# A remade order for the opening list of a fused attention and feed-forward kernel on one Trainium2 core

## The chip, the cores and the metric

The kernel runs on one core of one Trainium2 chip. The metric is the device time of one execution in microseconds (us); lower is better. The engines are TensorE (PE, with its weight loads as PEld), VectorE (DVE), ScalarE (ACT), GpSimd (POOL) and the sync engine (SP), which here only issues transfers (DMA). Each engine works through its own instructions in order.

## The reference

The kernel computes attention within chunks of 64 tokens, and on its result a feed-forward layer with a leaky rectifier:

```python
scores = scale * np.matmul(q_c, k_c.transpose(0, 1, 2, 4, 3))   # chunks of 64 x 64, scale = 1/8
scores = scores - np.max(scores, axis=-1, keepdims=True)
attn = np.exp(scores)
attn = attn / (np.sum(attn, axis=-1, keepdims=True) + 1e-09)
out = np.matmul(attn, v_c)                                      # 8 x 8 heads x 576 x 64
x = out.transpose(0, 2, 1, 3).reshape(4608, 512)
h = x @ w_in                                                    # 512 x 2048
g = np.maximum(h, 0.0) + alpha * np.minimum(h, 0.0)
y = g @ w_out                                                   # 2048 x 512
```

All inputs are float32. The weights w_in and w_out reach the chip as 64-bit floating point numbers, split in the kernel into 32-bit parts.

## The kernel before, in words

The 4608 tokens are cut into 36 sub-blocks of 128 tokens (two chunks, eight heads), and four sub-blocks form a block of 512 tokens. Every operand of a large product is kept as two parts, a high one rounded to TensorE's fp32r form and a low one, the rest; a product is then high by high, high by low and low by high. The first three blocks go through the feed-forward layer directly, the other six in pairs by a scheme with seven products instead of eight on quarters of the matrices (lines 588 to 871), for which combinations of the weights are made and stored on the way.

The change is in the opening of the kernel. There the attention of the first eight sub-blocks (0 to 3 form block 0, 4 to 7 block 1), the conversion of the first nine of sixteen slices of both weights, and the first feed-forward steps of blocks 0 and 1 are issued in an order that is written out by hand: the string `START` (line 28), whose tokens the function `start` (line 879) turns into instructions one after the other. Within `tc.manual_schedule` (line 930) each engine keeps exactly the order of the tokens that belong to it. After the list a scheduler orders the instructions; the TensorE order is fixed again from step 20 on (line 957).

A token is a letter or two and a number. For sub-block s:

- `q`, `k`, `v`: a load (line 544, 552). Two sub-blocks at a time from s = 2 on. q0 and q1 are issued by ScalarE, the others by SP. The room for q and k of 4 and 5 is that of 0 and 1, so that this load waits for S0 and S1.
- `S`: scores, 16 small fp32 products into PSUM (line 256). `m`: their maxima on VectorE (line 298). Then, in the usual way, `z` scales the maxima (a small VectorE operation, line 309), `e` is 16 instructions on ScalarE, eight exponentials with the maximum as bias and eight reads of the accumulated sum (line 313), and `a` adds 1e-9 to the sums on GpSimd. For a sub-block in `SUBTRACTED`, `z` subtracts the maxima from the scores on VectorE (line 302), `e` is one exponential over the whole sub-block (line 304), and `a` is a sum on VectorE and the addition (line 307, 317). `r` is the reciprocal, `n` the multiplication with it (line 321, 323).
- `T`: four transposes on TensorE (line 344), `p`: the copy out of PSUM on ScalarE (line 356). `V`: the product with v, 16 small products (line 360); `x`: the high part of x, a copy on ScalarE (line 373); `l`: its low part, a subtraction on VectorE (line 375).
- `W`: that many products of zeros (128x128) on TensorE (line 895); nothing reads them.

For a weight slice f, `wi` or `wo` with the number alone is the load of 512 KB (line 178, SP). The following letters are the steps of its conversion (`piece`, line 180): `b` the magnitude (ScalarE, for `wi0` VectorE), `k`, `h`, `u`, `v` four integer steps on VectorE, `i` the high part (ScalarE, for `wi0` VectorE), `j` the low part (VectorE). `HALVES` names the scratch tile of each slice.

For block b and slice f, `h` is the first layer's 12 products of 128x512 (line 416), `R` a Relu on ScalarE, `G` the rectify on VectorE, `gh` the high part on ScalarE, `gl` the low part on VectorE, and `o` the second layer's 12 products (line 450). So h00 is block 0, slice 0, and o16 block 1, slice 6. `K` copies one of block 0's four partial results out and stores it (line 467). The first block's first turn takes three slices, the second's nine (`TURNS`, line 91): h18, h03 and so on follow after the list.

`BANKS` says which PSUM banks S, T and V of a sub-block use: before, one of three pairs of banks (ps_a, ps_oa, ps_ob); T uses the first bank of a pair.

Of the kernel before, what the change touches and what calls it, by code (L numbers as in the profile page):

```python
# [19 lines left out]
def bits(pattern):  # L20
# [5 lines left out]


START = """
W8 q0 k0 k1 q1 q2 S0 W1 k2 m0 S1 W5 wi1 z0 m1 e0 wi0 z1 a0 e1 r0 S2 k4 n0 S3 m2 q4 wi1b z2 T0 W6 m3
e2 a1 z3 wi1k v0 wi0b r1 wi1h n1 wi2 p0 wi0k T1 a2 e3 wi0h r2 S4 W3 v2 wi0u n2 m4 q6 p1 V0 a3 z4  # L30
wi0v e4 T2 W4 k6 r3 wi0i wi1u wi0j wo4 wi1v x0 V1 n3 p2 wo0 l0 x1 V2 wi2b a4 l1 T3 x2 wo1 wi2k S5 p3
l2 wi1i V3 m5 v6 S6 r4 x3 z5 n4 e5 wi4 l3 h00 m6 v4 wi2h z6 wi1j e6 wi2u S7 wi3 a5 wi2v h01 m7 wo2
r5 R00 z7 n5 wo0b G00 wi5 wi2i T5 e7 wo0k wi2j h02 wi7 a6 wo0h r6 wo0u wo5 n6 p5 wo0v gh00 T6 wo1b
a7 T4 wo3 gl00 wo0i V5 r7 wo1k p6 wo0j x5 V6 n7 p4 l5 x6 T7 wo1h V4 l6 p7 wo1u x4 o00 R01 wo1v wo2b
G01 wo1i l4 gh01 wo1j R02 V7 gl01 o01 x7 wo2k G02 wi4b wi3b wo2h wo2u gh02 l7 h10 wo2v gl02 wo2i
wi3k wo2j wi4k wo4b o02 wi3h wi4h R10 wo4k wi4u K0 wi3u K1 G10 h11 wi4v gh10 wi3v wi4i gl10 K2 wi3i
wo4h wi4j K3 o10 wo4u wo5b wi3j R11 wo4v wi5b G11 wo4i wo6 h12 wo5k gh11 wo4j wi6 gl11 wo3b wo5h
wo3k wo5u wo8 o11 R12 wo3h wo5v wi8 G12 wo5i wo3u gh12 wo7 h13 wo5j gl12 wi7b wo3v wi5k wo3i wi7k
wi5h o12 R13 wo3j wi5u G13 wi5v gh13 h14 wi7h wi5i gl13 wi6b wi5j wi6k wi7u wi6h o13 R14 wi7v G14
wi7i wi6u gh14 wo6b wi6v h15 gl14 wi6i wo6k wi6j wi7j wo7b wo6h o14 wo7k R15 wo6u G15 wo6v gh15 wo7h  # L40
wi8b gl15 h16 wo6i wo7u wo7v wo6j wo7i wi8k o15 wo7j R16 wo8b G16 wi8h gh16 wi8u gl16 h17 wi8v wo8k
wi8i wi8j wo8h o16 R17 G17 wo8u gh17 wo8v gl17 wo8i wo8j
"""
# [12 lines left out]
LISTED = 18

# [2 lines left out]
def tile_local_attention_prelu_ffn(  # L60
# [63 lines left out]
    def place(name, shape, dtype):  # L124
        return sides[name[:2]][0].tile(shape, dtype, name=name)
# [15 lines left out]
    FREE = 12  # L141
    RAWS = 6
# [89 lines left out]
    def attn_load(s, parts="qkv"):  # L232
# [61 lines left out]
    def early_softmax(s, sc3):  # L294
# [412 lines left out]
    banks = ["ps_h", "ps_h", "ps_o0", "ps_o1", "ps_o2", "ps_o3"]  # L707
# [171 lines left out]
    def start(token):  # L879

        name, at = re.fullmatch(r"([a-zA-Z]+)(\d+)([a-z]?)", token).group(1, 2)
        s = int(at)
        if name in ("wi", "wo"):
            if token[-1].isdigit():
                fetch(name, s)
            elif token[-1] == "b":
                running[name, s] = piece(name, s, f"{name}{s}" in ALONE)
                next(running[name, s])
            else:
                next(running[name, s])  # L890
        elif name in ("q", "k"):
            first(("q", "k").index(name), s, 1 if s < 2 else 2, nc.scalar if token in ("q0", "q1") else nc.sync)
        elif name == "v":
            first_v(s)
        elif name == "W":
            hps = ps_h.tile([P, TB], F32, name="ps_h")
            for _ in range(s):
                nc.tensor.matmul(hps[:, :P], lhsT=plain, rhs=plain, start=True, stop=True)  # L898
        elif name == "S":
            running["softmax", s] = early_softmax(s, early_scores(s))  # L900
        elif name in ("m", "z", "c", "e", "a", "r", "n"):
            next(running["softmax", s])
        elif name == "T":
            running["transpose", s] = early_transpose(s)
            next(running["transpose", s])
        elif name == "p":
            next(running["transpose", s])
        elif name == "V":
            running["values", s] = early_values(s)
            next(running["values", s])  # L910
        elif name in ("x", "l"):
            next(running["values", s])
        elif name == "K":
            store(accs[0], 0, True, (s,))
        else:
            b, f = int(at[0]), int(at[1:])
            if name == "h":
                running["ffn", b, f] = first_layer(x[b], f)
                next(running["ffn", b, f])
            elif name in ("R", "G", "gh"):  # L920
                next(running["ffn", b, f])
            elif name == "gl":
                scored[b, f] = next(running["ffn", b, f])
            elif name == "o":
                if f == 0:
                    accs[b] = results()
                ffn_out(accs[b], scored.pop((b, f)), f, 0, (n0, n1)[b] - 1)
# [153 lines left out]
```

## Time and profile before

| | us |
|---|---|
| median of three runs | 770.79 |
| lowest and highest run | 770.68, 771.45 |
| span of the profiled execution | 770.2 |
| TensorE busy in it | 760.4 (99%) |
| VectorE busy | 646.7 (84%) |
| ScalarE busy | 447.3 (58%) |
| GpSimd busy | 184.8 (24%) |

The span goes from the first to the last instruction; of the profiled execution no other time is given than this span, which lies 0.6 us under the median of the runs. A busy share is an average over the whole span. Matmuls overlap, so that a row's duration (0.38 us for a 128x512 product) is longer than the distance from one to the next.

### The profile page before, as it was taken

The numbers are of one execution on the slowest core, as the hardware profiler recorded it, in microseconds if no ns is written. First come the engines' busy times: TensorE is split into PE (matmuls) and PEld (weight loads), VectorE is DVE, ScalarE is ACT, GpSimd is POOL, SyncE is SP. The second block draws the span as 40 slices with busy tenths as digits, with TensorE's granted clock in tenths as the row PEclk, the third lists the DMA queues.
The fourth block names the chain that finished last, engine by engine and source line by source line (L and its number), as shares of the span: only waits on it lengthen the run. The fifth ranks groups of instructions, "written<-read, shape, count | busy, mean of one in ns | idle before, by whom it ended". The sixth has DMA issues, their size and how long they took to land.

```text
span 770.2 us, 15415 instructions
## 1 busy us (share of the span) xinstructions
PE 760.4 (99%) x5558; PEld 639.8 (83%) x5558; DVE 646.7 (84%) x1140; ACT 447.3 (58%) x1221; POOL 184.8 (24%) x304
## 2 busy tenths in 40 slices
PE   7999999999999999999999999999999999999998
PEld 7788887888888888888888888888888888888886
DVE  6999988989899886877899898777898977679784
ACT  6975555576666665666657456664574544354643
POOL 1153322343254331111121121111221121122110
PEclk9999999999999999999999999999999999999999
DMA  9859496468798775878765678875656765555573
GB/s 349 337 196 386 176 324 216 163 229 226 234 238 274 240 258 200 304 275 277 263 234 197 233 250 288 269 239 206 207 193 223 260 228 193 204 205 192 198 258 144
DMA packets 69322, 184.52 MB, mean 240 GB/s; under 512 B 10992, under 2 KB 18176, under 8 KB 69120
## 3 DMA queue, kind: packets, MB, share of 16 engines
q0 software_dynamic: 34336, 119.56, 45.9%
q1 hardware_dynamic: 34480, 63.20, 24.2%
q8 instruction: 44, 0.72, 0.4%
q10 hardware_dynamic: 432, 0.79, 0.3%
q14 instruction: 30, 0.25, 0.1%
HBM read 135.27 MB, written 42.99 MB: 231 GB/s over the span
## 4 chain that ended last, share of the span: by engine, by line
PE 92%; ACT 4%; DVE 2%; DMA 2%; issue 0%; ACTq 0%; SPq 0%
PE ps_o L722 20%; PE ps_o L850 19%; PE ps_h L422 14%; PE ps_h L722 10%; PE ps_h L850 10%; PE ps_oa L458 8%; PE ps_ob L458 7%; PE ps_a L388 2%; PE ps_a L272 2%; ACT wi L313 1%; ACT wo L313 1%; DMA raw<-w_in 1%; DMA raw<-w_out 1%; PE ps_h L898 1%; ACT wi L207 0%
## 5 line engine op out<-in xcount | busy, mean ns | idle before, releaser
L422 PE MATMUL ps_h<-xh,wi 128*128 128x512 f32 x384 | 101.7, 385 | 0.7 <-DVE g L410 0.5
L422 PEld LDWEIGHTS ps_h<-xh,wi 128*128 128x128 f32 x384 | 70.7, 187 | 13.8 <-DVE g L410 0.9
L722 PE MATMUL ps_o<-wi,raw 128*128 128x512 f32 x336 | 79.1, 382 | 0.0
L722 PEld LDWEIGHTS ps_o<-wi,raw 128*128 128x128 f32 x336 | 62.5, 187 | 11.2
L678 ACT CAST gh<-wo 128x512 fp32r<-128x512 f32 x66 | 41.0, 620 | 47.4 <-PE ps_o L850 31.8
L287 ACT ACTIVATE pr<-ps_a,mx 128x64 f32<-128x64 f32 x224 | 67.2, 325 | 0.8
L458 PE MATMUL ps_oa<-wo,gh 128*128 128x512 f32 x192 | 58.5, 385 | 0.1
L458 PE MATMUL ps_ob<-wo,gh 128*128 128x512 f32 x192 | 57.7, 380 | 0.0
L422 PE MATMUL ps_h<-xl,wi 128*128 128x512 f32 x192 | 50.6, 381 | 0.0
L679 DVE TENSOR_TENSOR gl<-wo,gh 128x512 fp32r<-128x512 f32 x63 | 43.2, 686 | 7.5 <-ACT gh L678 7.1
L287 ACT ACTIVATION_READ_ACCUMULATOR pr<-ps_a,mx 128x1 f32 x224 | 48.6, 217 | 0.0
L659 POOL DMA_DIRECT2D raw<-wi_a x42 | 22.3, 531 | 102.1 <-PE ps_o L722 54.5
L659 POOL DMA_DIRECT2D raw<-wo_a x42 | 22.2, 529 | 90.8 <-PE ps_o L850 51.2
L407 ACT ACTIVATE wo<-gh 128x512 f32<-128x512 f32 x24 | 15.2, 632 | 48.5 <-DVE gh L752 48.5
L678 ACT CAST ta<-wo 128x512 fp32r<-128x512 f32 x42 | 26.1, 621 | 26.4 <-PE ps_o L850 15.2
L422 PEld LDWEIGHTS ps_h<-xl,wi 128*128 128x128 f32 x192 | 35.8, 187 | 6.7 <-DVE xl L375 0.2
L458 PEld LDWEIGHTS ps_ob<-wo,gh 128*128 128x128 f32 x192 | 35.9, 187 | 6.4
L458 PEld LDWEIGHTS ps_oa<-wo,gh 128*128 128x128 f32 x192 | 35.3, 187 | 7.0 <-ACT gh L436 0.5
L722 PE MATMUL ps_o<-wi,wo 128*128 128x512 f32 x168 | 40.4, 383 | 0.0
L722 PE MATMUL ps_o<-wi,wi 128*128 128x512 f32 x168 | 40.4, 383 | 0.0
L722 PE MATMUL ps_h<-wi,raw 128*128 128x512 f32 x168 | 40.4, 382 | 0.0
L407 ACT ACTIVATE g<-ps_h 128x512 f32<-128x512 f32 x48 | 29.5, 614 | 17.5 <-PE ps_h L422 17.5
(296 smaller groups left out, 2036.2 us busy)
## 6 DMA issues: line engine op xcount, KB each, us to landing
raw<-wi_a POOLq DMA_DIRECT2D x42, 512.0 KB, 4.4
raw<-wo_a POOLq DMA_DIRECT2D x42, 512.0 KB, 3.5
wi<-wi_a POOLq DMA_DIRECT2D x21, 512.0 KB, 3.7
wo<-wi_a POOLq DMA_DIRECT2D x21, 512.0 KB, 4.3
wi<-wo_a POOLq DMA_DIRECT2D x21, 512.0 KB, 3.5
wo<-wo_a POOLq DMA_DIRECT2D x21, 512.0 KB, 3.6
k_sb<-kT SPq DMA_DIRECT2D x28, 256.0 KB, 4.7
q_sb<-qT SPq DMA_DIRECT2D x28, 256.0 KB, 4.1
```

The source lines that it names most:

```text
L272: pe(nc.tensor.matmul(att[0][c * C:(c + 1) * C, par, (NP + hp) * C:(NP + hp + 1) * C], lhsT=q_sb[rows, 2 * hp + c], rhs=kb[rows, 2 * hp + ...
L287: last = nc.scalar.activation(pr[:, g], sc3[:, g // NP, g % NP], AF.Exp, bias=mx[:, g], scale=SCALE, accum_out=sm[:, g])
L313: last = nc.scalar.activation(pr[:, g], sc3[:, g % 2, g // 2], AF.Exp, bias=mx[:, g], scale=SCALE, accum_out=sm[:, g])
L388: pe(nc.tensor.matmul(att[0][par * C:(par + 1) * C, c, hp * C:(hp + 1) * C], lhsT=v_sb[rows, h * C:(h + 1) * C], rhs=p[rows, :, par * NP + ...
L407: nc.scalar.activation(g, h, AF.Relu, scale=-1.0)
L422: pe(nc.tensor.matmul(woven(hps), lhsT=wi[f][:, l, k * P:(k + 1) * P], rhs=woven(xx[:, k]), start=(i == 0 and k == 0), stop=(i == 2 and k ...
L458: pe(nc.tensor.matmul(woven(o), lhsT=a[:, ts], rhs=woven(wo[f][:, l]), start=(f == first and i == 0), stop=(f == last and i == 2),))
L659: streamed[0] = nc.gpsimd.dma_start(out=f32(t), in_=units[side][n])
L678: hi = nc.scalar.copy(t_hi, t)
L679: return hi, nc.vector.tensor_tensor(t_lo, t, f32(t_hi), op=ALU.subtract)
L722: pe(nc.tensor.matmul(woven(ps), lhsT=w[:, l, k * P:(k + 1) * P], rhs=woven(xx[:, xl]), start=first and at == 0, stop=at == n - 1, skip_gr ...
L850: pe(nc.tensor.matmul(woven(ps[m]), lhsT=w[:, l, m * P:(m + 1) * P], rhs=woven(xx), start=i in (1, 5, 2) and j == 0 and n == 0, stop=j == ...
```

## The change

The list gets another order. Eight products of zeros (W8) stand in front as before, but of the later ones 7 are left of 19. `SUBTRACTED` now holds sub-blocks 0, 2, 5 and 6 instead of 0 alone. For the sub-blocks in the new `REMAINDERS` (0 to 4), the low part of x is formed in PSUM: the high part, once copied out, is multiplied by a negated identity on TensorE and added to the bank (a new token `X`, two products of 128x256), and `l` is then a copy on ScalarE. The identity is negated once, on ScalarE. `BANKS` now counts single banks (a pair is two numbers), T may use either bank of a pair or a bank of ps_h (6 and 7), and one tile per pair serves all tokens. `HALVES` is remade with the order. The lists are cut here to the front, and the new one to the front, the middle that bears on block 1, and the end.

```diff
 START = """
-W8 q0 k0 k1 q1 q2 S0 W1 k2 m0 S1 W5 wi1 z0 m1 e0 wi0 z1 a0 e1 r0 S2 k4 n0 S3 m2 q4 wi1b z2 T0 W6 m3
-e2 a1 z3 wi1k v0 wi0b r1 wi1h n1 wi2 p0 wi0k T1 a2 e3 wi0h r2 S4 W3 v2 wi0u n2 m4 q6 p1 V0 a3 z4
-wi0v e4 T2 W4 k6 r3 wi0i wi1u wi0j wo4 wi1v x0 V1 n3 p2 wo0 l0 x1 V2 wi2b a4 l1 T3 x2 wo1 wi2k S5 p3
-l2 wi1i V3 m5 v6 S6 r4 x3 z5 n4 e5 wi4 l3 h00 m6 v4 wi2h z6 wi1j e6 wi2u S7 wi3 a5 wi2v h01 m7 wo2
...
-wi8b gl15 h16 wo6i wo7u wo7v wo6j wo7i wi8k o15 wo7j R16 wo8b G16 wi8h gh16 wi8u gl16 h17 wi8v wo8k
-wi8i wi8j wo8h o16 R17 G17 wo8u gh17 wo8v gl17 wo8i wo8j
+k0 q0 W8 S0 m0 k1 q1 z0 W1 S1 e0 q2 m1 k2 z1 a0 r0 e1 W1 S2
+n0 wi0 m2 S3 m3 z2 wi0b a1 q4 W1 T0 p0 k4 r1 z3 v0 wi0k k6 e2 n1
+W4 S4 wi0h e3 a2 T1 m4 q6 r2 p1 z4 S5 a3 n2 m5 e4 v2 r3 V0 x0
+z5 wi0u T2 V1 S6 X0 a4 n3 T3 p2 x1 wi0v l0 m6 r4 p3 z6 wi1 X1 V2
+wi0i V3 l1 wi1b x2 x3 n4 S7 wi0j wi1k m7 T4 wi1h X2 z7 wi2 v4 e5 l2 wi1u
+X3 a5 l3 wi1v h00 p4 wi2b r5 V4 wi2k wo0 n5 e6 wi1i e7 wo2 a6 wo0b a7 wi2h
+v6 x4 T5 p5 R00 r6 wi1j h01 X4 wo1 n6 r7 wi2u T6 l4 wi7 wi4 n7 wo0k wi2v
+wo0h T7 p6 V5 p7 G00 wo0u wi2i V6 wi2j V7 R01 x7 G01 x6 wo3 wo2b x5 gh00 wo1b
+l7 l6 l5 h02 wo0v h10 gl00 gh01 wo0i wo0j R02 wo1k G02 wi3 o00 gh02 wo1h wo2k wo1u h11
+wo2h wo1v wo2u gl01 wo1i wo1j wo4 o01 wi7b wi3b wo2v wo2i gl02 wo8 wi7k wo2j wi3k R11 R10 G11
+wi4b wi3h gh11 o02 wi5 wi7h G10 wi3u wi3v K2 gl11 wo5 h12 gh10 wi3i wi7u wi4k wi3j K3 wi5b
+h13 wi4h K0 K1 gl10 wi5k wi4u R13 wi5h wi4v wi5u wi7v R12 wi7i o10 o11 wi4i wi5v G12 wi5i
...
+wo6j o14 wi8b wo7k R16 G16 wo7h gh16 wi8k wo7u wo8b wi8h wo8k gl16 h17 o15 R17 wo8h wo8u wi8u
+wi8v wi8i wo7v wo8v G17 wo7i wo7j wo8i wo8j gh17 o16 gl17 wi8j
 """
-SUBTRACTED = (0,)
+SUBTRACTED = (0, 2, 5, 6,)
+REMAINDERS = (0, 1, 2, 3, 4,)
 BANKS = {
...
+    "S0": 4, "S1": 2, "S2": 0, "S3": 4, "S4": 0, "S5": 2, "S6": 0, "S7": 2, "T0": 2, "T1": 6, "T2": 7, "T3": 6, "T4": 7, "T5": 0, "T6": 1, "T7": 0, "V0": 4, "V1": 2, "V2": 4, "V3": 0, "V4": 4, "V5": 2, "V6": 4, "V7": 0,
 }
...
     make_identity(nc, ident)
+    minus = room(FREE + RAWS + 1, [P, P], F32R)
+    nc.scalar.mul(minus, ident, -1.0)
...
+    pairs = {}
+
     def banks_of(token):
-        pool, name = ((ps_a, "ps_a"), (ps_o, "ps_oa"), (ps_o, "ps_ob"))[BANKS[token]]
-        return pool.tile([P, 2, TB], F32, name=name)
+        pair, bank = divmod(BANKS[token], 2)
+        if pair == 3:
+            return ps_h.tile([P, TB], F32, name="ps_h")
+        if pair not in pairs:
+            pool, name = ((ps_a, "ps_a"), (ps_o, "ps_oa"), (ps_o, "ps_ob"))[pair]
+            pairs[pair] = pool.tile([P, 2, TB], F32, name=name)
+        return pairs[pair][:, bank] if token[0] == "T" else pairs[pair]
...
                 xo[to, c, cols], lhsT=v_sb[rows, h * C:(h + 1) * C], rhs=p[rows, h * C:(h + 1) * C],
+                start=hp == 0 or s not in REMAINDERS, stop=True, skip_group_check=hp > 0,
             ))
...
         nc.scalar.copy(xh, xo)
         yield
-        nc.vector.tensor_tensor(xl, xo, f32(xh), op=ALU.subtract)
+        if s in REMAINDERS:
+            for c in range(2):
+                pe(nc.tensor.matmul(banks[:, c, :NP * C], lhsT=minus, rhs=xh[:, c], start=False, stop=True, skip_group_check=True))
+            yield
+            nc.scalar.copy(xl, xo)
+        else:
+            nc.vector.tensor_tensor(xl, xo, f32(xh), op=ALU.subtract)
         yield
```

## Rows read from the trace of the kernel before

**Rows 1.** Stretches of 10 us: busy us (instructions) by engine; granted clock, DMA share, GB/s.
```profile
0.00:10.00 10.00, 8.83 (x156) 8.01 (x156) 3.81 (x10) 3.52 (x13) 1.60 (x8) 1.00 0.82 305
10.00:20.00 10.00, 6.71 (x125) 5.72 (x121) 9.64 (x24) 10.00 (x61) 1.29 (x4) 1.00 1.01 398
...
30.00:40.00 10.00, 9.40 (x137) 7.75 (x137) 9.54 (x20) 9.68 (x31) 0.59 (x1) 1.00 0.51 205
40.00:50.00 10.00, 10.00 (x76) 8.24 (x74) 9.97 (x20) 6.29 (x12) 5.75 (x9) 1.00 0.34 118
```

**Rows 2.** TensorE's timeline at o00, h18 and the later wait.
```profile
37.80 0.72 PE L458 MATMUL ps_oa<-wo,gh 128*128 128x512 f32 x2
...
86.30 1.04 PE L422 MATMUL ps_h<-xh,wi 128*128 128x512 f32 x4
...
126.74 1.15 PE L422 MATMUL ps_h<-xh,wi 128*128 128x512 f32 x4 [0.50 <-DVE g L410]
```

**Rows 3.** The chain of waits (start, us, what): V7, a block, 98 to 127 us.
```profile
40.73 0.62 PE ps_a L367 x32
...
49.50 2.64 PE ps_h L422 x12
...
98.38 0.59 ACT q_sb L492
...
101.27 7.06 DMA raw<-w_in
...
126.02 0.67 DVE g L410
```

**Rows 4.** ScalarE's timeline, 0 to 45 us.
```profile
7.42 0.63 ACT L304 ACTIVATE wo<-wo 128x512 f32<-128x512 f32 x1 [4.75 <-DVE wo L302]
8.60 0.31 ACT L313 ACTIVATE wo<-ps_ob,mx 128x64 f32<-128x64 f32 x1 [0.55 <-DVE mx L309]
...
28.62 0.70 ACT L407 ACTIVATE g<-ps_h 128x512 f32<-128x512 f32 x1
29.10 0.82 ACT L194 ACTIVATE tb<-wo 128x512 f32<-128x512 f32 x1
29.70 0.72 ACT L207 CAST wi<-tc 128x512 fp32r<-128x512 f32 x1
30.21 0.43 ACT L313 ACTIVATE wi<-ps_oa,mx 128x64 f32<-128x64 f32 x1
...
32.53 0.75 ACT L356 COPY wo<-ps_ob 128x512 f32<-128x512 f32 x1
```

**Rows 5.** VectorE's timeline: the list's first operation, wo0's low part, the list's end, a wait.
```profile
5.97 0.69 DVE L298 TENSOR_REDUCE mx<-ps_oa 128x8 f32<-128x512 f32 x1 [4.96 <-PE ps_oa L261]
...
34.92 0.69 DVE L209 TENSOR_TENSOR wo<-tb,wo 128x512 fp32r<-128x512 f32 x1
...
82.91 0.69 DVE L209 TENSOR_TENSOR wi<-tb,wi 128x512 fp32r<-128x512 f32 x1 [0.35 <-ACT wi L207]
...
87.25 0.69 DVE L209 TENSOR_TENSOR wo<-ta,wo 128x512 fp32r<-128x512 f32 x1
87.86 0.42 DVE L196 TENSOR_SCALAR tc<-tc 128x512 f32<-128x512 f32 x1
88.19 0.42 DVE L196 TENSOR_SCALAR tb<-tb 128x512 f32<-128x512 f32 x1
...
102.96 0.69 DVE L209 TENSOR_TENSOR wo<-tc,wo 128x512 fp32r<-128x512 f32 x1 [1.25 <-ACT wo L207]
```

**Rows 6.** The sync queue's timeline: the load of k4.
```profile
7.60 0.33 SPq L548 DMA_DIRECT2D wo<-kT  x1
```

**Rows 7.** TensorE's timeline: products of zeros, and scores that waited for a load.
```profile
1.06 3.78 PE L898 MATMUL ps_h<-wo 128*128 128x128 f32 x16 [1.06 <-DVE table L147]
...
11.64 1.50 PE L898 MATMUL ps_h<-wo 128*128 128x128 f32 x12
...
15.06 0.69 PE L261 MATMUL ps_ob<-wo,wo 64*64 64x64 f32 x32 [0.34 <-DMA wo<-qT]
```

More of the change, by code (lines that the diff above doesn't have):

```diff
@@ L28 @@
 START = """
-W8 q0 k0 k1 q1 q2 S0 W1 k2 m0 S1 W5 wi1 z0 m1 e0 wi0 z1 a0 e1 r0 S2 k4 n0 S3 m2 q4 wi1b z2 T0 W6 m3
-e2 a1 z3 wi1k v0 wi0b r1 wi1h n1 wi2 p0 wi0k T1 a2 e3 wi0h r2 S4 W3 v2 wi0u n2 m4 q6 p1 V0 a3 z4
-wi0v e4 T2 W4 k6 r3 wi0i wi1u wi0j wo4 wi1v x0 V1 n3 p2 wo0 l0 x1 V2 wi2b a4 l1 T3 x2 wo1 wi2k S5 p3
-l2 wi1i V3 m5 v6 S6 r4 x3 z5 n4 e5 wi4 l3 h00 m6 v4 wi2h z6 wi1j e6 wi2u S7 wi3 a5 wi2v h01 m7 wo2
-r5 R00 z7 n5 wo0b G00 wi5 wi2i T5 e7 wo0k wi2j h02 wi7 a6 wo0h r6 wo0u wo5 n6 p5 wo0v gh00 T6 wo1b
@@ L34 @@
[L34 to L39, printed above, removed]
@@ L40 @@
-wi7i wi6u gh14 wo6b wi6v h15 gl14 wi6i wo6k wi6j wi7j wo7b wo6h o14 wo7k R15 wo6u G15 wo6v gh15 wo7h
-wi8b gl15 h16 wo6i wo7u wo7v wo6j wo7i wi8k o15 wo7j R16 wo8b G16 wi8h gh16 wi8u gl16 h17 wi8v wo8k
-wi8i wi8j wo8h o16 R17 G17 wo8u gh17 wo8v gl17 wo8i wo8j
+k0 q0 W8 S0 m0 k1 q1 z0 W1 S1 e0 q2 m1 k2 z1 a0 r0 e1 W1 S2
+n0 wi0 m2 S3 m3 z2 wi0b a1 q4 W1 T0 p0 k4 r1 z3 v0 wi0k k6 e2 n1
+W4 S4 wi0h e3 a2 T1 m4 q6 r2 p1 z4 S5 a3 n2 m5 e4 v2 r3 V0 x0
+z5 wi0u T2 V1 S6 X0 a4 n3 T3 p2 x1 wi0v l0 m6 r4 p3 z6 wi1 X1 V2
@@ new lines @@
+h13 wi4h K0 K1 gl10 wi5k wi4u R13 wi5h wi4v wi5u wi7v R12 wi7i o10 o11 wi4i wi5v G12 wi5i
+wi4j wi7j wo7 wi5j wo3b gh12 wi6 wo3k gl12 wo3h wi6b G13 wo3u wi8 wi6k h14 wo4b wo6 wo3v gh13
+wi6h gl13 wi6u wo3i wo3j h15 wo4k wi6v wo5b wo5k o12 o13 wi6i R14 wo5h wo4h wi6j wo4u G14 h16
+wo5u wo6b gh14 wo4v wo4i wo6k gl14 R15 wo6h wo4j wo7b wo5v wo6u G15 wo6v wo5i wo5j gh15 gl15 wo6i
+wo6j o14 wi8b wo7k R16 G16 wo7h gh16 wi8k wo7u wo8b wi8h wo8k gl16 h17 o15 R17 wo8h wo8u wi8u
+wi8v wi8i wo7v wo8v G17 wo7i wo7j wo8i wo8j gh17 o16 gl17 wi8j
@@ L43 @@
 """
 ALONE = ('wi0',)
-SUBTRACTED = (0,)
+SUBTRACTED = (0, 2, 5, 6,)
+REMAINDERS = (0, 1, 2, 3, 4,)
 HALVES = {
-    "wi1": "ta", "wi0": "tb", "wi2": "tc", "wo0": "tb", "wo1": "ta", "wo2": "tc", "wi4": "tb", "wi3": "ta",
-    "wo4": "tc", "wo5": "tb", "wi5": "ta", "wo3": "tc", "wi7": "tb", "wi6": "tc", "wo6": "ta", "wo7": "tc",
-    "wi8": "tb", "wo8": "ta",
+    "wi0": "ta", "wi1": "tb", "wi2": "tc", "wi3": "tc", "wi4": "tb", "wi5": "tc", "wi6": "ta", "wi7": "ta", "wi8": "tb", "wo0": "ta", "wo1": "tc", "wo2": "tb", "wo3": "tb", "wo4": "tc", "wo5": "tb", "wo6": "ta", "wo7": "tc", "wo8": "ta",
@@ L51 @@
 }
 BANKS = {
-    "S0": 1, "S1": 2, "S2": 0, "S3": 1, "T0": 2, "T1": 0, "S4": 2, "V0": 1, "T2": 0, "V1": 2, "V2": 0, "T3": 1,
-    "S5": 2, "V3": 1, "S6": 0, "S7": 1, "T5": 2, "T6": 1, "T4": 2, "V5": 0, "V6": 1, "T7": 2, "V4": 0, "V7": 0,
+    "S0": 4, "S1": 2, "S2": 0, "S3": 4, "S4": 0, "S5": 2, "S6": 0, "S7": 2, "T0": 2, "T1": 6, "T2": 7, "T3": 6, "T4": 7, "T5": 0, "T6": 1, "T7": 0, "V0": 4, "V1": 2, "V2": 4, "V3": 0, "V4": 4, "V5": 2, "V6": 4, "V7": 0,
 }
@@ L346, in early_transpose @@
         pr = probs.pop(s)
-        tp = banks_of(f"T{s}")[:, 0]
+        tp = banks_of(f"T{s}")
         for hp in range(NP):
@@ L367, in early_values @@
             pe(nc.tensor.matmul(
-                xo[to, c, cols], lhsT=v_sb[rows, h * C:(h + 1) * C], rhs=p[rows, h * C:(h + 1) * C], start=True, stop=True,
+                xo[to, c, cols], lhsT=v_sb[rows, h * C:(h + 1) * C], rhs=p[rows, h * C:(h + 1) * C],
+                start=hp == 0 or s not in REMAINDERS, stop=True, skip_group_check=hp > 0,
             ))
         yield
-        xo = by_chunk(xo)
+        banks, xo = xo, by_chunk(xo)
         xh, xl = (tokens(t, s) for t in x[s // SPB])
@@ L910, in start @@
             next(running["values", s])
-        elif name in ("x", "l"):
+        elif name in ("x", "X", "l"):
             next(running["values", s])
```

## The prediction

> **What bounds the kernel now.** I read the busy time by stretches first. From 40 us on TensorE is busy all the time; before that it isn't, and VectorE and ScalarE are full instead: in the stretches from 10 to 20 and from 30 to 40 us each works 9.5 us or more of the ten [rows 1]. So the time is the moment from which TensorE runs without a break, plus the matmuls still to do. TensorE's timeline gives the moment: o00 starts at 37.80 [rows 2], V7 follows (0.62 us [rows 3]), and after that one feed-forward block of 12 products comes upon another. A block takes 2.64 us [rows 3]. h18, the first block after the list, starts at 86.30 [rows 2]. Check: from 37.80, V7 and the 18 blocks between (o00 to o02, h10 to h17, o10 to o16) make 0.62 + 18 x 2.64 = 48.14, so 85.94; 0.36 goes into hand-overs.
>
> Then I read the chain of waits for a later place where TensorE is short, since a lead that is won early must get past it. There is one: at 126.74 it has waited 0.50 us for VectorE's rectify [rows 2, 3]. That chain hangs on TensorE itself: the end of the second block's first turn at 98.35, ScalarE's copies of the results from 98.38, a weight load that the sync queue can issue only at 101.27 and that takes 7.06 us, and then a second load and its conversion [rows 3]. On the way VectorE idles, as the 1.25 us at 102.96 show [rows 5].
>
> **ScalarE's part.** Prices, by the distance from one start to the next: sixteen exponentials of a sub-block 2.32 us (30.21 to 32.53), a magnitude 0.60, a cast of weights 0.51, a Relu 0.48 [rows 4]; a copy out of PSUM I take at the Relu's 0.48, as it reads the same tile. The exponential of a subtracted sub-block is one instruction of 0.63 [rows 4]. Three more sub-blocks are subtracted: 3 x (2.32 - 0.63) = 5.1 less. Five low parts come over from VectorE: 5 x 0.48 = 2.4 more. In all 2.7 less.
>
> With the new order the sum has to be laid out anew. ScalarE begins e1 at 8.60 in both kernels, since W8, S0, W1 and S1 stand in the same order. From there to the end of p7, which V7 needs, stand: e1, e3, e4, e7 (9.28); e2, e5, e6 (1.89); eight p, five x, five l (18 x 0.48 = 8.64); wi1b, wi2b, wo0b (1.80); wi1i (0.51); R00 (0.48). That is 22.60, so 31.2. Two waits come on top. e2 needs z2, which VectorE reaches after n0, m2 and m3 at about 12.0, while p0 ends at 11.4: 0.6. e4 needs z4, behind m4, behind S4, which waits for q4 and k4. Their load can be issued only at 7.60, when S1 has freed the room [rows 6]; in the kernel before S4 waited for q4 until 15.06 [rows 7]. Now one weight of 512 KB instead of two stands ahead of them, so they land about 1.3 us earlier (512 KB at the 398 GB/s of the stretch from 10 to 20 us [rows 1]), at some 13.8, but part of that may go where the queue now runs dry at 8 us: wait of 0 to 0.9, taken 0.4. p7 then ends at 32.2, V7 at 32.9.
>
> **TensorE's part.** After V7 stand h02, h10, o00 and the rest with no attention between. h00 and h01 fall before, at about 23 and 27. So TensorE is continuous from h02 at 32.9, with 19 blocks to h18: 32.9 + 19 x 2.64 + 0.36 = 83.4 instead of 86.30. **Lead: 2.9 us.** The ten new products by the negated identity (X0 to X4) are 128x256; before has nothing of that form. They cost between 22 ns (a 64-column product, 0.69 us for 32 [rows 7]) and 220 ns (a twelfth of a block); I take 110, nearest by columns to the latter. They lie in the part in which TensorE idles, and ScalarE has other work between each x and its l. Of the zeros' products, 12 fewer, nothing is gained: TensorE idles there anyhow. The new bank numbers put V1 behind z5, S6 behind e4, S7 behind l1 and V7 behind p7; only the last is on the path, and it is counted. The negation of the identity falls into ScalarE's idle 4.75 us ahead of 7.42 [rows 4]: nothing, unless it stands ahead of q1's issue, which would then wait for the identity and bring S1 up to 0.9 late. GpSimd's softmax steps fall from seven to four; none was waited for.
>
> **VectorE's part.** It gains three subtractions (0.60 each), three sums with their addition (0.70) and loses three scalings (0.10) and five low parts (0.60): +3.6 - 3.0 = +0.6. A tally of the whole list by start-to-start prices (0.60 for a 512-column operation as from 87.25 to 87.86, 0.34 for a one-operand integer step as the next, 0.10 for a small one [rows 5], 0.66 for a rectify by its row of 0.67 [rows 3]) is 76.5 before and 77.1 after. Before, the list runs from 5.97 to 87.86 [rows 5], 81.9: 5.4 is lag, 3.0 of it ahead of wo0's low part (34.92, tally 26.5). Laying the new order out, I find 1.8 there (bounds 1.4 and, as before, 3.0) and keep the other 2.4. The list then ends at 5.97 + 77.1 + 4.2 = 87.2 (86.4 to 88.5) instead of 87.86. So VectorE is only about 0.6 ahead where TensorE is 2.9 ahead. In between the conversions and splits still meet their blocks: h13 (51) has its weights at 51 to 52, needed for its last third at 53; o16 at 80.5 has its low half at about 80.6, for its third product at 80.9, which is close. The stores of K0 to K3 go out at 49 to 52 and have five weight loads behind them on the sync queue (wo5, wo7, wi6, wi8, wo6); the first of these weights is converted at some 65 by the tally: nothing.
>
> **What is late next.** The new list ends with wi8's low part, which h18 needs for its last four products, 8 x 0.22 = 1.76 us after its start: 85.2 against 87.2. Before, that part was done at 83.6, and wo8's was last (87.25) [rows 5]. If h03's products are put between, TensorE waits for nothing: their bank comes free with G17, 2.4 before the end of the list, at 84.8. If not, it waits 2.0. Before, the products around 88 and 90 us are mixed between blocks just so, thus I take a third of it, 0.7. Lead kept: 2.2. The chain from 98.35 to 126.74 begins with TensorE's own end and moves with it, as far as VectorE's idle time there, 1.25 and more, lets it follow (0.6 + 1.25 = 1.85 at least, against 2.2): I take 2.1. After that nothing idles on TensorE up to 765 us, so the 2.1 stay. Span 770.2 - 2.1 = 768.1; the median of the runs shown is 770.79, 0.6 above the span, so **768.7 us**. Around it 767.9 to 769.2.
>
> **Rivals.** *VectorE decides.* If the lag ahead of wo0's low part stays at 3.0, the list ends at 88.5, and TensorE, with nothing to put between, stands at h18 until VectorE is there; the lead shrinks to what VectorE has, between -0.6 and +1.5. For it speaks that VectorE is full from 10 us on and gets 0.6 us more to do; against it that the front of the new list has fewer steps in which VectorE waits for ScalarE. 770.2 (769.3 to 771.4). 0.24.
>
> *The whole lead is kept*, 2.9 to 3.3, if the products are mixed well and the later loads come early: 767.5 to 767.9. 0.08.
>
> *TensorE's clock falls* (the one on the other side). [...] 0.10. [...]
>
> *The front is bound by loads*, not by ScalarE: then the new exponentials only wait, and nothing moves, 770.8. For it: DMA is full from 10 to 20 us [rows 1]; against it: one wait of TensorE for a load [rows 7], and ScalarE full. 0.05.
>
> **How the numbers follow.** The forecast has 0.53. A measurement of this kernel can tell 0.2%, 1.5 us, from no change: faster is below 769.25, slower above 772.3 (the clock's case lies on that edge and is put there whole). Faster 0.53 + 0.08 = 0.61, same 0.24 + 0.05 = 0.29, slower 0.10. The range 767.3 to 771.0 takes in the forecast, the whole lead and most of VectorE's case; the clock and a little at either end stay out.
>
> **What would show it.** Right: h02 near 33 and no idle TensorE from there to h18 near 83.5; p7 ending near 32; ScalarE's exponentials of sub-blocks 2, 5 and 6 single instructions of about 0.6 us; VectorE's last low part near 87; the wait near 124 longer than 0.5. Wrong: h02 later than 35; a TensorE wait of 2 us or more at wi8; zeros' or block products at twice their time after 10 us; S4 later than 15.

## The result, and the profile after

| us | before | after |
|---|---|---|
| median of the runs side by side | 771.12 | 776.01 |
| lowest and highest | 770.68, 772.02 | 774.42, 778.07 |
| span of the profiled execution | 770.2 | 773.9 |
| start of h02 | 30.84 | 36.80 |
| start of h18 [rows 2] | 86.30 | 87.39 |
| end of the list's low parts of weights on VectorE [rows 5] | 87.94 | 90.96 |

The ratio is 1.0062, 95% interval 1.0049 to 1.0075: 4.9 us slower, where 768.7 was forecast. Two runs that took far longer than all others, one of e1 (2005.72 us) and one of before beside e7 to e9 (1308.42), are left out of the ratios, and e1's out of its median. In the new order V4 to V7 stand ahead of h02, in the old one behind it, so that the row of h02 compares unlike places.

Of the profiled execution of after the device time is known too: 775.71, 1.8 us above its span. If as much lies above before's span, its profiled execution took about 772.0, an estimate; that is before's longest run (772.02), and would be why the spans differ by 3.7 us and the medians by 4.9.

TensorE's timeline of after (start us, us, what, xcount, idle before it and what ended it):

```profile
14.35 0.69 PE L271 MATMUL ps_a<-wo,wo 64*64 64x64 f32 x32 [1.89 <-DVE ta L201]
...
21.89 0.58 PE L377 MATMUL ps_ob<-wi,wi 64*64 64x64 f32 x25 [0.36 <-issue]
...
28.43 0.45 PE L377 MATMUL ps_ob<-wo,wo 64*64 64x64 f32 x14 [0.48 <-issue]
...
34.48 0.55 PE L377 MATMUL ps_a<-wi,wi 64*64 64x64 f32 x22
36.49 0.39 PE L377 MATMUL ps_a<-wi,wi 64*64 64x64 f32 x10 [1.46 <-issue]
36.80 1.16 PE L439 MATMUL ps_h<-xh,wi 128*128 128x512 f32 x4
...
42.21 0.60 PE L475 MATMUL ps_oa<-wo,gh 128*128 128x512 f32 x2
...
87.39 1.15 PE L439 MATMUL ps_h<-xh,wi 128*128 128x512 f32 x4
...
94.54 1.05 PE L439 MATMUL ps_h<-xh,wi 128*128 128x512 f32 x4
97.14 1.16 PE L439 MATMUL ps_h<-xh,wi 128*128 128x512 f32 x4 [1.54 <-DVE g L427]
...
135.64 0.71 PE L475 MATMUL ps_oa<-wo,gh 128*128 128x512 f32 x2 [1.27 <-ACT gh L453]
```

Between 36.8 and 87.4 TensorE has no break, as forecast, but it begins 3.9 us later than forecast. It then waits 1.54 us at 97.14 and 1.27 at 135.64, where before waited only 0.50 [rows 2]. So 1.09 (h18) + 1.54 + 1.27 - 0.50 = 3.4 of the 3.7 us between the spans; 0.3 is spread out.

The row at 14.35 names VectorE for its 1.89 us, but traces with the same instructions ahead of it show another cause: S4 starts 0.09 us after the load of k4 has landed (e2: landed 14.40, S4 14.49; e5: 13.56 and 13.65; e8: 12.20 and 12.29). This load takes 5.1 to 6.4 us in the three, so S4 comes up to 2.2 us earlier or later from execution to execution, with no edit ahead of it. Its landing in after's own trace is not recorded.

The row at 36.49 is the strange one. V7, 32 small products, stops after 22 of them for 1.46 us, and nothing is shown that it waited for ("issue"). V2 and V4 stop in the same manner. In the same stretch the profile lists, besides the queues with data, one of the kind "instruction" (packets, MB, share of 16 engines; 18 to 40 us):

```profile
q8 instruction: 4, 0.07, 1.1%
```

Each packet has 16,384 bytes. They run from 19.44 to 20.45, 26.11 to 27.02, 34.04 to 34.92 and 37.78 to 38.72 us, and TensorE goes on, behind its stops, 1.44, 1.41 and 1.57 us after the end of the first three. That these packets bring TensorE's program, and that the stops are waits for it, was my assumption, from the kind's name and these times.

ScalarE's timeline of after:

```profile
11.61 0.59 ACT L366 COPY wo<-ps_oa 128x512 f32<-128x512 f32 x1 [0.76 <-PE ps_oa L359]
...
15.67 0.59 ACT L366 COPY wo<-ps_h 128x512 f32<-128x512 f32 x1 [0.47 <-PE ps_h L359]
16.73 0.32 ACT L323 ACTIVATE wo<-ps_a,mx 128x64 f32<-128x64 f32 x1 [0.47 <-DVE wi L333]
...
32.40 0.59 ACT L390 CAST xl<-ps_ob 128x512 fp32r<-128x512 f32 x1 [0.48 <-PE ps_ob L388]
33.33 1.08 ACT L366 COPY wi<-ps_a 128x512 f32<-128x512 f32 x2 [0.34 <-PE ps_a L359]
...
36.91 0.59 ACT L384 CAST xh<-ps_a 128x512 fp32r<-128x512 f32 x1 [1.49 <-PE ps_a L377]
...
65.56 0.70 ACT L197 ACTIVATE ta<-wi 128x512 f32<-128x512 f32 x1 [3.06 <-DMA wi<-w_in]
```

VectorE's timeline of after, which answers to [rows 5]:

```profile
37.53 0.69 DVE L392 TENSOR_TENSOR xl<-ps_a,xh 128x512 fp32r<-128x512 f32 x1 [1.23 <-ACT xh L384]
...
41.25 0.69 DVE L212 TENSOR_TENSOR wo<-ta,wo 128x512 fp32r<-128x512 f32 x1 [0.26 <-ACT wo L210]
...
66.30 0.43 DVE L199 TENSOR_SCALAR ta<-ta 128x512 f32<-128x512 f32 x1 [1.32 <-ACT ta L197]
...
90.27 0.69 DVE L212 TENSOR_TENSOR wi<-tb,wi 128x512 fp32r<-128x512 f32 x1
...
96.34 0.74 DVE L427 SCALAR_TENSOR_TENSOR g<-g,rise,ps_h 128x512 f32<-128x512 f32 x1
```

V7's stop is handed on: x7 waits for V7, l7 waits for x7, and wo0's low part, in front of which the prediction counted lag, comes at 41.25 instead of 34.92. The last low part, wi8's, ends at 90.96. h18's last four products (94.54) come behind o17, its rectify only at 96.34, and h04, the next block, needs its bank: 1.54 us.

### The profile page after: what moved, and what is told of

Same layout as the page of the kernel before. It is cut to its first block, busy times and chain, and to the rows that moved or that the text cites. A ratio compares the mean times of both kernels' runs of the same rounds, so it can differ in the third digit from the quotient of the medians.

```text
span 773.9 us, 15365 instructions
## 1 busy us (share of the span) xinstructions
PE 759.0 (98%) x5544; PEld 638.2 (82%) x5544; DVE 647.2 (84%) x1141; ACT 445.2 (58%) x1182; POOL 183.1 (24%) x301
## 3 DMA queue, kind: packets, MB, share of 16 engines
q1 hardware_dynamic: 34480, 63.20, 24.6%
## 4 chain that ended last, share of the span: by engine, by line
PE 87%; DVE 6%; DMA 3%; ACT 2%; issue 1%; SPq 0%; ACTq 0%
PE ps_o L739 19%; PE ps_o L867 19%; PE ps_h L439 12%; PE ps_h L739 10%; PE ps_h L867 10%; PE ps_oa L475 6%; PE ps_ob L475 6%; PE ps_a L405 2%; PE ps_a L282 2%; DMA raw<-w_in 1%; DMA wi<-w_in 1%; ACT wo L323 1%; DVE gl L456 1%; DMA partial<-v_sb 1%; DVE wo L212 0%
## 5 line engine op out<-in xcount | busy, mean ns | idle before, releaser
L453 ACT CAST gh<-g 128x512 fp32r<-128x512 f32 x48 | 30.1, 629 | 17.1 <-DVE g L427 10.7
```

Source lines behind the costliest of these rows:

```text
L453: nc.scalar.copy(gh, g)
```

## The experiments

The zeros' products that some of these kernels leave out or add are read by nothing; every kernel computes the whole output. The theory at the outset had three parts: the packets of the kind "instruction" stop V7, the stores K0 to K3 hold up weight loads, and wi8's place at the end of the list costs the wait at 97.

**e1, seven zeros' products fewer.** It moves every later product 14 places forward in TensorE's program (an fp32 product of zeros counts two: W8 is 16 records [rows 7]). The lines are cut on the right.

```diff
-k0 q0 W8 S0 m0 k1 q1 z0 W1 S1 e0 q2 m1 k2 z1 a0 r0 e1 W1 S2
-n0 wi0 m2 S3 m3 z2 wi0b a1 q4 W1 T0 p0 k4 r1 z3 v0 wi0k k6 e2 n1
-W4 S4 wi0h e3
+k0 q0 W8 S0 m0 k1 q1 z0 S1 e0 q2 m1 k2 z1 a0 r0 e1 S2
+n0 wi0 m2 S3 m3 z2 wi0b a1 q4 T0 p0 k4 r1 z3 v0 wi0k k6 e2 n1
+S4 wi0h e3
```

> The changed kernel without its seven later products of zeros (14 fewer rows on TensorE ahead of V2). Theory A, TensorE's instruction loads: in the changed kernel TensorE stops without any wait shown after 7 rows of V2 (0.36 us), 18 rows of V4 (0.48) and 22 rows of V7 (1.46), 127 rows apart, each time 1.4 to 1.6 us after an instruction packet of 16 KB has come in. With 14 rows fewer these stops move 14 rows on: out of V7 into h02, out of V4 into T5; V7's stop of 1.46 is gone, x7 comes 1.0 to 1.5 us earlier, VectorE's list ends 0.8 to 1.5 earlier, time 774.5 to 775.3. Rival C, the zeros hold TensorE's clock: small products after 10 us take about 1.0 us a sub-block instead of 0.65, time above 777. Rival D, only VectorE's added work counts: no change, 776.

774.50 us (three runs, 774.03 to 774.99), ratio 1.0045 (1.0029 to 1.0062). TensorE's timeline of e1:

```profile
33.05 0.67 PE L377 MATMUL ps_a<-wi,wi 64*64 64x64 f32 x32
33.65 1.16 PE L439 MATMUL ps_h<-xh,wi 128*128 128x512 f32 x4
35.33 1.04 PE L439 MATMUL ps_h<-xl,wi 128*128 128x512 f32 x4 [0.53 <-issue]
...
95.48 1.15 PE L439 MATMUL ps_h<-xh,wi 128*128 128x512 f32 x4 [1.52 <-DVE g L427]
```

V7 is whole, and the stop sits 14 products later, after h02's fourth: 10 more of V7 and 4 of h02. It is the place in the program that stops, not V7's data. h02 comes 3.15 us earlier, h18 (85.73) only 1.66, and the wait behind h18 stays. In exchange the granted clock reads 0.50 from 7.9 to 18.1 us.

**e2, the loads of wo5, wo7 and wi6 ahead of K2** (lines cut on the right).

```diff
-wi4b wi3h gh11 o02 wi5 wi7h G10 wi3u wi3v K2 gl11 wo5 h12 gh10
+wi4b wi3h gh11 o02 wi5 wi7h G10 wi3u wi3v wo5 wo7 wi6 K2 gl11 h12 gh10
...
-wi4j wi7j wo7 wi5j wo3b gh12 wi6 wo3k
+wi4j wi7j wi5j wo3b gh12 wo3k
```

> The changed kernel with the loads of wo5, wo7 and wi6 issued ahead of the copy and store K2 instead of behind K2 or K0 and K1. Theory B, loads behind the stores: wi6's load, issued at 58.9 and landed at 65.5, made ScalarE wait 3.06 us and VectorE 1.32; issued near 48 it is there by 56, ScalarE takes wi6's magnitude near 62.5, VectorE's idle 1.32 is gone, its list ends 1.0 to 1.3 earlier, time 774.7 to 775.2. Rival: something else is late there at once, VectorE stays full but its list ends no earlier, 776.

776.02, 1.0066 (1.0051 to 1.0081): nothing gained. VectorE's idle time between 60 and 70 us did go from 1.32 us to 0.00, but V7's stop took 2.20 in the profiled execution, the longest of the four (777.14), and the clock fell behind it. TensorE's timeline of e2, and then its stretch behind the stop (us, busy us and count of PE, PEld, DVE, ACT, POOL; granted clock, DMA share, GB/s):

```profile
37.05 0.39 PE L377 MATMUL ps_a<-wi,wi 64*64 64x64 f32 x10 [2.20 <-issue]
```

```profile
37.90:41.30 3.40, 3.40 (x9) 2.65 (x8) 2.95 (x5) 3.40 (x8) 2.45 (x5) 0.50 0.26 88
```

So this run can't price the stores alone. It shows that they were the cause of the idle 1.32 us. In its trace V7's stop, 0.74 us longer, and the granted clock of 0.50 behind it took more back; what the other three runs did was not seen.

**e3, both.**

> Both edits together. A and B: the two gains are of VectorE's idle time at different places and add up: list end 2 to 2.8 earlier, time 773.2 to 774.2, still above the kernel before since VectorE's waits between 10 and 40 us stay. Rival: the sum is no better than one of them, 775.

773.56, 1.0030 (1.0017 to 1.0043). h18 starts at 84.66, 1.6 us ahead of before, and the list ends at 87.33, as the prediction had it (87.2). But the lead is lost behind it: 1.47 us at h04, 0.82 ahead of 132.3, and 1.27 ahead of 192.7, there for a load of pT in a later block's attention. Against e1, which lacks the loads' edit alone (774.03 to 774.99), e3's runs (772.83 to 773.98) lie 0.9 us lower by the medians, just without overlap: that is what the loads' edit gave there. A lead of 1.6 us at h18 is no gain while wi8 is last.

**e5, wi8's steps earlier at the end of the list, all else as after.**

```diff
-wi8b wo7k R16 G16 wo7h gh16 wi8k wo7u wo8b wi8h wo8k gl16 h17 o15 R17 wo8h wo8u wi8u
-wi8v wi8i wo7v wo8v G17 wo7i wo7j wo8i wo8j gh17 o16 gl17 wi8j
+wi8b wo7k R16 G16 wo7h gh16 wi8k wo7u wo8b wi8h wo8k gl16 h17 o15 R17 wi8u wo8h wi8v
+wi8i wo7v wi8j wo8u G17 wo7i gh17 wo7j gl17 o16 wo8v wo8i wo8j
```

> The changed kernel with wi8's last steps moved ahead of wo7's, wo8's and gl17 at the end of the list, where the kernel before has them; wo8's low part is last. Theory E, the end of the list: with wi8's low part last, h18's last four products come behind h03 and o17, h18's bank is freed late, and h04 waits for its Relu and rectify (1.54 us at 95.6 us, and 1.5 in all three variants run so far, wherever TensorE stands). With wi8 earlier h18 runs in one piece and that wait goes: time 774.3 to 774.8. Rival F, VectorE is simply behind there: the wait stays, or comes elsewhere before 130 us, and the time is 776.

773.21 (770.99 to 777.36), 1.0030 (1.0015 to 1.0045): 2.8 us less than after, the most that one edit gave and 1.1 less than theory E had, though h18 starts where it did (87.36) and V7 stops for 1.40 us. The wait at h04 is gone, and so is the one of 1.27; one wait is left behind h18, where after has 1.54 + 1.27. TensorE's timeline of e5:

```profile
122.51 1.16 PE L439 MATMUL ps_h<-xh,wi 128*128 128x512 f32 x4 [0.68 <-DVE g L427]
```

**e6, the three edits together.**

> e3_both with the same end of the list. E: 1.5 us less than e3_both, 771.8 to 772.3. F: as e3_both, 773.5.

770.88 against 771.08, ratio 0.9997 (0.9988 to 1.0005), below both theories. All that the change lost is back, and nothing more. The granted clock of its runs is 0.993 to 0.998; in its profile it is 0.50 from 9.3 to 19.5 us. That profile is of the longest of its eleven runs (772.91). In it h18 is only 0.55 us ahead of before, and TensorE's longest wait behind it is for a load of pT, a wait that e3 (1.27) and e7 (0.52) have too, but before and after have not. TensorE's timeline of e6:

```profile
85.75 1.04 PE L439 MATMUL ps_h<-xh,wi 128*128 128x512 f32 x4
...
120.72 1.15 PE L439 MATMUL ps_h<-xh,wi 128*128 128x512 f32 x4 [0.47 <-DVE g L427]
...
191.65 0.63 PE L405 MATMUL ps_a<-pT,v_sb 64*64 64x64 f32 x27 [1.40 <-DMA pT<-t]
```

**e7, e6 with 12 places fewer than after instead of 14, and some zeros' products in a wider form** (128x512; `wide` is a tile of zeros). The loads and the end of the list are e6's; the front is shown against after, cut on the right.

```diff
-k0 q0 W8 S0 m0 k1 q1 z0 W1 S1
+k0 q0 W4 U1 S0 m0 k1 q1 z0 S1
...
-W4 S4 wi0h e3
+U2 S4 wi0h e3
...
+        elif name in ("W", "U"):
+            n = P if name == "W" else TB
...
+                nc.tensor.matmul(hps[:, :n], lhsT=plain, rhs=wide[:, :n] if name == "U" else plain, start=True, stop=True)
```

> The kernel with three edits, with zeros' products put back in another form: fewer and wider (128x512), 6 instructions fewer in front, two wide ones ahead of S4, so that 12 rows are left out of the changed kernel's own count instead of 14. Theory (the pauses between small products cost the clock in the opening, and what stops V7 is the place of the 127th row, not the zeros as such): granted clock 1.00 throughout, S4 to V1 at full speed (scores of 32 rows about 0.7 us instead of 1.1), no stop of TensorE inside V7, h02 at 33.5 to 34.5, and 769.3 to 770.6, a little faster than the three edits' 770.9. Rival (the half speed up to 19 us lies in time in which TensorE idles anyhow): 770.6 to 771.2, no different.

772.1, 1.0014 (1.0005 to 1.0023): neither. V7 is whole and the clock holds up to 24.6 us, as the theory had it, but an earlier stop grew. TensorE's timeline of e7:

```profile
20.26 0.56 PE L379 MATMUL ps_ob<-wi,wi 64*64 64x64 f32 x19
23.03 0.39 PE L379 MATMUL ps_ob<-wi,wi 64*64 64x64 f32 x11 [2.21 <-issue]
```

The stop in V2 falls after 19 products instead of 7: 12 places, as many as were left out. It takes 2.21 us instead of 0.36, again ending 1.37 us after a packet (20.67 to 21.66), and the clock is at 0.50 from 24.6 to 28.0, behind it. h02 is back at 36.57. That was in neither theory. TensorE reached V2 0.94 us earlier than in after (20.26 against 21.20), but the packet also began 1.23 us later (20.67 against 19.44); why it did stays open. And the profile is of one of the longest of eleven runs (773.58), so that a stop of 2.21 is not shown for the median.

**e8, the loads and the end of the list, zeros' products as in after.**

> The changed kernel with the three loads ahead of the stores and with wi8's steps earlier at the end of the list, all its zeros' products kept. Theory: V7's stop (1.4 us) stays, h02 near 36.5, h18 at 86 to 87, no wait of 1.5 us near 95; 771.8 to 773.2, about 1 to 2 us behind the three edits. Rival (the zeros make no difference once VectorE's list is shorter): 770.5 to 771.3.

772.03 (769.44 to 774.57), 1.0009 (0.9993 to 1.0024): in the theory's range, but the interval overlaps that of e6, so that the zeros' part by itself is not settled. TensorE's timeline of e8 shows four stops:

```profile
14.86 0.39 PE L271 MATMUL ps_oa<-wo,wo 64*64 64x64 f32 x10 [0.54 <-issue]
...
21.65 0.58 PE L377 MATMUL ps_ob<-wi,wi 64*64 64x64 f32 x25 [1.14 <-issue]
...
27.94 0.46 PE L377 MATMUL ps_ob<-wo,wo 64*64 64x64 f32 x14 [0.27 <-issue]
...
35.39 0.39 PE L377 MATMUL ps_a<-wi,wi 64*64 64x64 f32 x10 [0.86 <-issue]
```

After 22 products of S5, 7 of V2, 18 of V4 and 22 of V7. The last three are the places of after, 0.36, 0.48 and 1.46 us there: the places are fixed, the lengths vary from trace to trace, e8's by execution alone, since it has after's instructions up to there. The runs of after, e5 and e8 also lie further apart (3.7, 6.4 and 5.1 us from lowest to highest) than those of e6 and e7 (2.9 and 2.0), in whose traces V7 is whole; but e2's, with a stop of 2.20, lie within 1.9. Whether the stop's length does this from run to run was not seen, as each kernel has one trace. The granted clock, which is known for each run, may tell a part: in after the two runs at 1.000 took 774.42 and 775.71, those at 0.995 and 0.997 took 776.31 and 778.07; in e5 the six at 0.999 and above took 770.99 to 773.77, the four below 773.36 to 777.36. In e8 there is no such order (769.44 at 0.997).

**e9, before without its 19 later zeros' products** (W1, W5, W6, W3, W4 taken out of its list).

> The kernel before without its 19 later zeros' products (W1, W5, W6, W3, W4), order and all else kept. Theory of the clock: pauses of 1 to 3 us between small products then hold nothing, the granted clock falls to half in the stretch from 7 to 20 us, small products there take 1.1 instead of 0.7 us a group, and the time is 0 to 1.5 us above before. Rival: the granted clock stays 1.00 and the time is before's or up to 0.5 below it.

772.95, 1.0019 (1.0010 to 1.0028): 1.5 us slower. Two stretches of e9:

```profile
10.00:20.00 10.00, 5.76 (x88) 4.35 (x92) 9.34 (x23) 9.98 (x59) 1.13 (x4) 0.50 1.03 416
20.00:30.00 10.00, 9.76 (x215) 7.98 (x208) 9.02 (x20) 9.07 (x42) 1.43 (x3) 0.85 1.03 415
```

The granted clock is 0.50 from 9.4 to 23.0 us, where before had 1.00 [rows 1]. It fell behind a pause of 1.94 us that ended at 8.56. o00 and h18 both come 0.78 us later than in before.

**e4, the new order with the low parts of x on VectorE** (all X taken out, `REMAINDERS = ()`, W9 for W4: ten products more there for the ten taken out, so that V7 keeps its place in the program).

> The changed kernel with the five low parts back on VectorE (no X, REMAINDERS empty; nine products of zeros for four ahead of S4, so that TensorE's count of rows stays). If VectorE's list decides the time, its five subtractions (3.0 us) bring its end 1.5 to 3 later: 777.5 to 779. If ScalarE or TensorE decides the front, five copies (2.4 us) and ten products fewer bring V7 0.5 to 2 earlier and the time to 774 to 775.5.

776.85, 1.0077 (1.0061 to 1.0094), outside both theories and no different from after within the intervals. The trace is of its shortest run (774.91; the others took 776.69 to 777.21). In it the price moves: h00 waits for VectorE,

```profile
26.83 1.17 PE L439 MATMUL ps_h<-xl,wi 128*128 128x512 f32 x4 [2.93 <-DVE xl L392]
...
34.99 0.67 PE L377 MATMUL ps_a<-wi,wi 64*64 64x64 f32 x32
```

but V7 is whole, at the same place of the program: the packet that in after ended at 34.92, inside V7, ended here at 31.70, 3.3 us ahead of it. h02 starts at 35.59 and the list ends at 90.23. So in the new order the runs tell neither a gain nor a loss by X: what one engine is spared another waits for.

**b1, before with `SUBTRACTED = (0, 2, 5, 6)` alone.**

> The kernel before, in its own order, with sub-blocks 0, 2, 5 and 6 subtracted on VectorE. VectorE gets 3.6 us more in its list, ScalarE 5.1 less. If VectorE decides: list end 2 to 3.6 us later, time 773 to 774.5. If ScalarE decides the front, as I took it: o00 up to 3 us earlier, time 768 to 770.5.

773.28, 1.0033 (1.0023 to 1.0043). The stretches of b1 show the reason:

```profile
10.00:20.00 10.00, 6.69 (x130) 5.90 (x134) 9.86 (x25) 7.92 (x41) 0.66 (x3) 1.00 1.03 417
20.00:30.00 10.00, 9.19 (x205) 7.22 (x196) 9.94 (x19) 6.50 (x12) 0.00 (x0) 1.00 1.02 414
```

ScalarE gets free (7.92 and 6.50 us), VectorE has hardly any idle time (9.86 and 9.94 us busy), and both o00 (39.37) and the list's end (89.49) come 1.6 us later. In the old order VectorE decides, and the subtraction is a loss.

**b2, before with the low parts of sub-blocks 0 to 4 in PSUM alone**, each X just ahead of its l.

> The kernel before, in its own order, with the low parts of x of sub-blocks 0 to 4 formed in PSUM (X right ahead of each l). VectorE 3.0 us less, ScalarE 2.4 more. If VectorE decides: list end 1.5 to 3 us earlier, time 769 to 770.5. If ScalarE decides the front: o00 1 to 2.4 us later, time 772 to 773.5.

777.58, 1.0080 (1.0065 to 1.0094), outside both theories. Its o00 comes at 41.59, 3.8 us late. TensorE's timeline of b2:

```profile
29.07 1.17 PE L432 MATMUL ps_h<-xl,wi 128*128 128x512 f32 x4 [1.47 <-ACT xl L383]
```

Now TensorE waits for ScalarE, and VectorE works only 5.03 us from 20 to 30 us. The granted clock was at 0.50 from 15.3 to 18.7 us here too, with all products of zeros in place. This is one placing of X; others weren't tried in the old order.

## Why the prediction was wrong

**The step that failed is ScalarE's part with TensorE's start from it**: "p7 then ends at 32.2, V7 at 32.9". p7 ended at 34.4 and V7 at 36.8. Of the 3.9 us, 2.2 are ScalarE's: from 8.36 to 34.4 it worked 23.4 us (22.6 were counted) and idled 2.6 (1.0 counted). The wait ahead of e4 was sized right (0.47 against 0.4), though S4 came 0.5 us later than taken. Those for T0, T1, X4 and T6 or T7 (0.76, 0.47, 0.48 and 0.34 in the rows above) were not laid out. I had summed the engine that seemed to be full and taken its partners as ready. Another 1.46 us are V7's stop, which no row of before showed; e1 confirms that its place in the program makes it. The remaining 0.2 is spread out. 2.9 of lead less 3.9 is 1.0 late; measured, h18 is 1.09 late.

**VectorE's lag.** Taken as 1.8 us ahead of wo0's low part, bounds 1.4 to 3.0. In the new order the tally up to that step is 30.5, so it measured 41.25 + 0.6 - 5.97 - 30.5 = 5.4. V7's stop accounts for 1.23 of it, handed on through x7 and l7; the longest of the other waits are for ScalarE's casts of weights (0.74 at 34.95) and for scores (0.39 at 15.10). That it was the lag and not the work is seen in the stretch of the list, before and after (us, busy us and count of PE, PEld, DVE, ACT, POOL; granted clock, DMA share, GB/s):

```profile
5.97:87.94 81.97, 77.47 (x810) 65.09 (x811) 79.27 (x157) 61.76 (x191) 23.44 (x34) 1.00 0.80 301
```

```profile
5.97:90.96 84.99, 77.65 (x804) 64.98 (x805) 79.33 (x158) 58.65 (x151) 20.49 (x32) 1.00 0.78 285
```

VectorE is busy for 79.27 us in the one and 79.33 in the other; it idles for 2.70 and 5.66, and that makes the list end 3.0 later. With V7 whole and the loads first (e3) the list ended at 87.33, near the 87.2.

**"Thus I take a third of it, 0.7"**, for wi8 being last, was wrong in kind. h18 itself didn't wait, since its last products were put behind o17; h04, which needs h18's bank, did, 1.54 us. Mixing products between blocks moved the wait and did not take it away. e5 shows its price best: 2.8 us by the medians, with the later wait of 1.27 that went with it.

**K0 to K3: "nothing".** wi6's load, issued at 58.88 behind the stores, made ScalarE wait up to 65.56 (3.06) and VectorE 1.32. e2 took away the idle time without a gain, beside a longer stop of V7; e3 against e1 puts the price at 0.9 us, with the seven zeros' products left out in both.

**The rivals.** VectorE deciding (770.2) was nearest in mechanism for the old order, as b1 shows, but not for the change. The clock's case (772.3) rested on two blocks of the opening, h00 and h01, at half speed; no run shows both so. In its place e1, e3, e6 and e9 show a granted clock of 0.50 when zeros' products go (from 7.9 to 18.1, 8.6 to 12.0, 9.3 to 19.5 and 9.4 to 23.0 us), in e9 back at 1.00 ahead of h00 (24.89), e9 a price of 1.5 us, and e7 a slowed h00 behind its stop: the first four products took 1.91 us, 1.06 in after. In after's profile, with the 7 that remain, it was at 1.00 throughout, so it isn't what made the change slow there; in the two runs at 0.995 and 0.997 it may have had a part. The loads' case (770.8) had a part too: S4, which e4 waits for, waited for the load of k4. No case that I listed reached 776, since each had only one thing late. The range's upper end, 771.0, came from a sum in which unlisted waits had no room.

**Right**: the price of a subtracted exponential (0.63 to 0.69 us), of the low part's copy (0.48), of the negation (nothing); TensorE continuous from h02 on; S4 earlier than before (14.35 against 15.06, though 13.8 was taken), by the luck of a load that varies by more than this difference. The products by the negated identity took 0.12 (X3, X4) to 0.25 us (X1) each from start to start, where 0.11 was taken.

**Why repairing it only came out even** (e6) is not settled. VectorE's work in the list is the same before and after (79.27 and 79.33 us), so the list's end has little to gain, and ScalarE's 2.7 us were freed beside an engine that had no room; b1 supports this for the old order. But in e6's own trace, of its longest run, TensorE waited only 0.47 us for VectorE and 1.40 for a load of pT near 192. No run moved those loads, and no run took VectorE's work alone away.

## What to carry to other kernels

When several engines are full at once, taking work from one moves the end only by the room that the others have; sum all of them with their waits before counting a lead, and follow the lead to the next bank, load and rectify that must be early too. In these kernels TensorE stopped inside bursts of small products, at fixed counts of its program: look for stops with "issue" as cause and for packets of the kind "instruction" just before them, and try another count of instructions, then look whether another stop grows, as in e7. Products of zeros are not free to remove: here the granted clock fell to 0.50 in the opening without them (e1, e3, e6, e9), though once with them too (b2, from 15.3 to 18.7 us).

## What the runs showed of the hardware that I had not expected

- The stops of TensorE come at counts of its program, whatever stands there. Counted in the traces from the start of the kernel, each stop of after and e1 to e8 from V2 on comes after 345 or 346, 472 or 598 products. In after and e8, with a weight load for each product and the semaphore instructions in between, the stops lie 255 to 257 instructions apart. TensorE has 11,421 instructions in the whole trace of after, 44.6 times 256, the middle of these, and queue q8 brought 44 packets, so that one packet for each such stretch would fit, an estimate:

```profile
q8 instruction: 44, 0.72, 0.4%
```

- Each of these stops ended 1.3 to 1.6 us after a 16,384-byte packet. In before the packets come as often (they begin at 20.11, 25.98, 33.70 and 38.10), but TensorE comes to the 346th, 473rd and 599th product only at 22.43, 29.16 and 37.47, 1.3, 2.3 and 2.9 us after the ends of the first three (21.14, 26.90, 34.60), and no such stop is shown. 32 products of V take 0.51 us (33.97 to 34.48 in after), so 127 of that kind would take 2.0, less than the packet and the time after it (0.9 + 1.4 to 1.6); an estimate that fits, and no more. What sets the time of a packet was not found.
- The clock fell to 0.50 behind stops of 2.2 us (e2 at 37.9, e7 at 24.6), and h02 then took 4.4 us instead of 2.7 (e2); behind after's 1.46 us it stayed at 1.00.
